# A list of kernel steps searched anew, and warm-up products of 256 instead of 512 columns

## The chip, the cores and the metric

The kernel runs on one core of a Trainium2 chip. The core's engines work side by side, each through its own queue in order: PE (matrix products; PEld is its loading of weights), DVE (vector operations), ACT (scalar functions and copies), POOL and SP. SP has no arithmetic here; it issues most of the transfers. The metric is the time of the program on the device in microseconds. Three runs of the kernel before took 153.74, 154.20 and 155.04 us, a median of 154.2.

## What is computed

Two models see the same input x (2048 positions of 512 values), and a gate mixes them:

```python
def _A_ref(x, ...):                    # state space: 512 complex states
    Lam_bar = jnp.exp(dt * Lam)
    Bu = jnp.einsum("bld,pd->blp", x + 0j, B_bar)
    for t in range(L):
        h = Lam_bar[None, :] * h + Bu[:, t, :]
    y = 2.0 * jnp.einsum("blp,dp->bld", hseq, Cmat).real + x * Dskip
def _B_ref(x, wqkv, w_phi, wo):        # linear attention: 32 heads of 16
    phi_q = concat(softmax(pq), softmax(-pq)); phi_k = the same of pk
    kv = einsum("bhsf,bhsd->bhfd", phi_k, v); z = sum of phi_k over s
    o = (phi_q @ kv) / (phi_q . z + 1e-6)
    return o.reshape(B, S, D) @ wo
g = sigmoid((x * gate_w).sum(-1, keepdims=True))
return g * a + (1 - g) * b
```

## The kernel before

The kernel has no scheduler that decides while it is built. It is written as some 190 small generators, called steps, and a string `ORDER` names them one after the other. A loop at the end reads the string: each token runs its generator up to the next `yield`, and what it issues there goes to the end of the queue of its engine. So the string is the order of every instruction on every engine. A token may carry the numbers of the PSUM banks that it takes (`k5@6`) and a `D` (`f0:D`), which sends a copy or a scaling to DVE instead of ACT. The banks are eight, with 2 KB in each partition. When a bank or a buffer is used again, the framework adds the wait for the earlier user; so it does between any two engines that use one bank.

The steps that the text speaks of:

- `Z` (L333 to L337): a product of zeros with zeros that nobody reads. It keeps PE busy in the head while the first loads are on their way.
- `Lk`, `Lx`, `Lv`, `Lb`, `Lq`, `Lc` (L226 to L259): loads, each issued by SP: rows of the key weights (two; the rest comes through ACT's queue at L159), two natural x tiles (L232) and seven transposing x loads of two tiles each (L236), value weights, state space matrices B, query weights, C.
- `W` (L315 to L323): key weights transposed by PE, and copied out; `f` (L469 to L479): four folds of them with the feature map, each ended by a copy; `w` the same for the queries. `T` (L325 to L331): transposes of the two natural x tiles.
- `V`, `P`, `U`, `P2` to `P4`, `M`, `i`: parameters of the state space, small vector operations on DVE with a few sines and exponentials on ACT.
- `k`, `v`, `q` (L528 to L551): projections of a tile of 128 positions, four products each, with a copy by ACT behind them (L135, the line of the helper `evac`). A `q` has three tokens: products, copy, and a DVE operation (L550) that takes the gate column from the same bank, as `nge`.
- `x`, `n`, `e`, `s` and `X`, `N`, `E`, `S`: the two softmaxes of up to four tiles: maxima and differences, minima and differences (DVE), exponentials (ACT, L589), sums and scaling (DVE); `S` ends with transposes by DMA. `a` adds keys times values on PE.
- `b`, `g`, `z`, `sa`, `sb`, `H`, `XX`, `hd`, `hk`, `ek`, `dp`: the state space, as products over strides of the sequence and corrections. `z` scans (L720) and multiplies again (L723); `c` scales C, `C` stores it turned.
- `y`, `o`, `O`, `t`, `R`: output of a tile. `y` is the state space's product, `o` the attention's with its division (L891), `O` its transpose by DMA (L904), `t` the product with `wo` into the same bank as `y` and the copy out (L922), `R` the store.

What a `q` does behind its four products, and `Z`:

```python
        evac(xrel(n), pq[:, 0:DF].rearrange("p (hh x) -> p hh x", hh=8))
        yield
        VS(out=nge[:, n:n + 1], in0=pq[:, DF:DF + 1], scalar1=-Z_MAX, scalar2=-1.0, op0=ALU.max, op1=ALU.mult)
        yield
```

Of the kernel before, what the change touches and what calls it, by code (L numbers as in the profile page):

```python
# [23 lines left out]
ORDER = """
Z@0 B Lx Lk Z Lk B Z Z B Z T0@1 T0 W01@2 Z W00@3 W00 Lx W10@1 W11@4 Lv B W10 Z W01 W11 Z T1@1 B f3@0 W00 T1:D W01 Lx
f2@3 V@2 f0@4 V Lx f3 P f1@5 f1 f0:D P P2 v0@1 P2 P2 Lb f2 k0@4 P2 P2 P U v1@5 k0 P4 V2@3 P3 P2 U k1@0 P4 k1 U k2@2
P4 P3 i i k0 k1 M i M v0 Lx k4@4 x0 i Lx k3@1 n0 x0 k7@0 n0 M i M2 Lb Lx V2 k5@6 k6@3 n0 x0 Lq Da k4 v3@4 x0 k2 k3
M2 n0 k9@1 x0 n0 i k11@2 x1 k8@7 k6:D L n1 x1 k5 n1 e0 k10@3 Da v3 x1 Lq n1 w2@4 k7 k9 v1 s0 Lb Lx n1 Db x1 k8 s0 w2
x1 U n1 Lb w3@1 x2 s0 k11 x2 Lx v6@0 w1@7 b10@5 n2 v6 M2 e1 w0@2 x2 s0 k10 n2 x2 s0 b01@0 b31@4 b30@6 n2 x2 w3 Lc n2
Db x0z s0 b00@3 g10@1 w0 k13@2 b30 x3 n2 b01 g00@0 x3 Da Lo s1 b10 Db b00 k13 w1 e2 g00 k14@2 Lc s1 n3 s1 k12@7 v5@3  # L30
g01@5 k12 g31@7 s0 g30@6 g30 gw e2 g00 c0:D s1 g10 x3 n3 b31 s1 g30 s2 Da Lc b20@4 k15@6 s1 g31 s2 k14 g10 a0@12 g01
c0:D c1 b20 x3 Lc a0 n3 k15 c2:D g01 v5 q3@0 c2:D s2 Lb g31 x3 c1:D q2@3 n3 c2 g31 x4 g01 s2 q3 x4 v2@6 g01 q2 s2 q2
g31 q3 n3 v4@4 g01 s2 s1 g20@0 n4 x4 g31 n4 v2 e3 Ld b21@3 g20 s2 a1 g31 b11@6 g31 c0:D s2 n4 g20 g01 a1 g31 b21 c3
q0@0 g11@3 v4 g21@4 b11 q0 g01 g11 g01 c3:D g31 q1@7 e3 q1 g11 x4 n4 g01 c0 x4 q6@6 q6 g21 q1 a2 g21 c3 s3 q0 b40@5
g11 n4 b50@0 g11 g21 c2 g21 v7@7 b40 g11 N0 g21 Lb X0 g11 a2 b50 s3 v10@0 g21 X0 q4@5 c1 g11 g21 v10 c1 g11 v7 N0 Ld
s3 a2 g21 g50@0 g11 a2 q4 g50 N0 g21 c3 q7@4 s3 z0@3 G0 X0 e4 z0 X0 s3 q5@7 N0 e4 q6 C g40@6 q4 q5 b70@5 X0 z0 C q5
N0 q7 C z0 s4 z0 g40 b60@3 b70 b71@7 b51@5 g40 q7 z0@4 b71 N1 z0 z0 s4 b41@7 X1 g70@4 z0 X1 b60 s3 g50 b41 g41@0 E0
b51 sa0@7 g60@3 s4 g70 sa0 sb0@7 s3 g60 s4 g71@5 sb0 E0 g41 g51@6 H0@7 s4 X1 g51 g70 g51 s4 S0 H0 C g71 H1@4 S0 X1
g60 g41 XX0 S0 g51 hd0 g41 H1 g71 G0 g51 b61@7 g71 N1 S0 v8@3 s4 g71 v9@4 b61 G1 g51 g61@7 G1 v8 XX0 g51 g41 g61 hd0
N1 a3 v9 g61 g71 s3 g71 g41 g41 a3 S0 v11@4 a3 g51 Ld hd1 g51 g41 S0 g61 g61 S0 g71 q10@3 v11 hd0 g61 g61 s4 a3 g71  # L40
XX0 N1 XX0 q10 g71 g41 g61 q11@4 g41 g61 v12@0 S0 g61 g51 z1@6 S0 q11 X1 N1 z1 hd0 z1 q8@7 q10 q8 q9@5 z1 q8 q13@3
q11 z1 v14@4 z1@7 v12 q9 q9 z1 S0 E1 E1 a4 hd1 X2 N2 z1 q12@5 v15@7 G0 G1 z1 N2 X2 N2 sa1@0 v13@6 sa1 q15@0 v13
sb1@6 S1 v14 hd0 v15 X2 S0 a4 S1 sb1 q14@4 H2@7 q12 G2 H3@6 S1 X2 q12 q14 hd1 S1 a4 q13 S1 H2 hd1 q14 a4 q13 Y Y Y
hd1 S1 hk4 S1 y1@5 Y END y0@3 o0@1 q15 y2@4 H3 N2 X2 o1@6 hk6 q15 o1 o1 XX1 o0 N2 hd0 y3@0 o0 o0 o1 y1 XX1 hk5 XX1
o3@1 o2@6 hd1 E2 o2 y3 X3 y2 o3 XX1 S1 o2 o3 hk4 S1 o2 y1 y0 o3 N3 hk5 E2 hk7 hk4 O0 y0 X3 S1 t0 y4@1 hk5 X3 t0 hk6
y2 hk5 hk7 X3 S2 hk4 t1 y3 hk7 o4@2 o5@6 N3 ek0 S2 t1 o5 o4 O1 o5 t2 y7@5 t3 hk6 S1 S2 hk7 S2 o4 o4 N3 o5 O2 t2 ek0
y5@4 N3 o7@6 hk6 S2 S2 o6@2 y4 y4 t3 ek1 ek3 y5 S2 ek0 X3 o6 dp6@0 y7 S2 y5 ek1 ek2 N3 o6 o7 ek0 o6 R1 t4 t5 ek1 ek2
o7 E3 o7 y6@2 ek3 t4 y7 S2 dp6 y6 ek1 S2 ek2 ek3 ek2 E3 o8@0 o8 ek3 ek6:D o8 ek4:D ek4 o9@6 o9 y6 t5 ek6:D ek7 ek4
o9 O3 y11@3 S3 o8 ek6 ek5 ek5 S2 t7 R0 R2 o9 t6 y10@4 y9@0 ek7 t6 O4 ek4 ek5 o10@6 o10 o10 ek7 ek5 y8@1 ek6 ek7 y11
dp1@2 S3 o10 S3 dp1 y9 o11@6 t7 G2 S3 G2 y8 o11 dp3@2 dp2@5 o11 o11 S3 t8 S3 dp7@6 dp0@7 O5 S3 dp2 S3 dp5@5 dp0 dp3  # L50
t9 dp5 y10 y14@2 S3 S3 dp4@5 S3 u8 t11 dp7 y12@7 u9 t10 dp4 o12@5 o12 t8 R3 o12 t9 u10 y12 y12 o13@0 R4 o12 t10 y14
o13 o13 y14 o13 o15@5 u11 y13@4 o15 o15 o14@0 o14 o15 y13 O6 G3 o14 O8 G3 y15@56 y13 t11 y15 o14 O7 y15 t13 t12 R5
G3 t12:D t13 R6 t14 t15 t14 R7 t15 R8 t15 t15:D R8
"""
# [20 lines left out]
def kernel(  # L75
# [237 lines left out]
    MM = nc.tensor.matmul  # L313
# [17 lines left out]
        yield  # L331

    def st_Z():  # L333
        pz = bank([P, D], F32, "pz")
        while True:
            MM(out=pz[:], lhsT=warm[:, 0:P], rhs=warm[:], start=True, stop=True)
# [664 lines left out]
```

## Time and profile before

| | |
|---|---|
| median of three runs | 154.2 us (153.74 to 155.04) |
| the profiled execution | 153.31 us |
| its span, first to last instruction | 151.6 us |
| instructions | 2814 |
| PE products | 978 |
| moved by DMA | 19.73 MB in 54109 packets |
| read from and written to HBM | 3.56 MB and 2.10 MB |
| granted TensorE clock, mean | 0.997 |

A row of the profile names a line of the kernel, the engine, the operation, and what it writes and reads; then the count and the time. A matrix product is pipelined: its row's duration is longer than the distance to the next one, so the busy time of PE is not its speed. An arrow `<-` behind an idle time names what ended it. A wait is put down to what came last by the profile.

### The profile page before, as it was taken

The page shows a single profiled execution, that of the slowest core. Times are in us where ns is not written, and L with a number is a line of the kernel's source. Part 1 is how long each engine was busy: PE and PEld are TensorE (multiplying, and loading weights), DVE is VectorE, ACT ScalarE, POOL GpSimd, SP SyncE. Part 2 cuts the span into 40 slices and gives each one's busy share as a digit, 9 for nine tenths or more (in the row PEclk, how much of TensorE's full clock was granted, in tenths as well). Part 3 has the DMA queues.
Part 4 walks back from the last instruction along what each step waited for, and adds up shares of the span by engine and source line. Part 5 has one row for each costly group of instructions (what it writes and reads, how often), then busy time and mean ns, then how long its engine had stood idle before and what let it go on. Part 6 is the DMA issues. An engine that isn't in the chain of part 4 may idle for free.

```text
span 151.6 us, 2814 instructions
## 1 busy us (share of the span) xinstructions
PE 141.1 (93%) x978; PEld 72.6 (48%) x978; DVE 135.7 (89%) x334; ACT 122.1 (81%) x239; POOL 19.5 (13%) x47
## 2 busy tenths in 40 slices
PE   6799999999999999979999999899998999989990
PEld 2444444444535555434556455445553554436640
DVE  2679999999999999699999999999999999999620
ACT  3599999999999999969898899999999994003240
POOL 7700885000000000000030006300000000000000
PEclk9999999999999999999999999999999999999998
DMA  3999999998200000910355924989968993797543
GB/s 74 318 231 210 188 181 199 232 196 159 74 0 0 0 0 5 237 41 0 76 132 88 213 49 69 161 155 200 181 38 192 210 198 62 106 181 203 104 119 123
DMA packets 54109, 19.73 MB, mean 130 GB/s; under 512 B 44496, under 2 KB 54096, under 8 KB 54096
## 3 DMA queue, kind: packets, MB, share of 16 engines
q1 hardware_dynamic: 51904, 18.19, 60.3%
q0 software_dynamic: 1248, 1.06, 4.7%
q10 hardware_dynamic: 944, 0.31, 0.8%
q8 instruction: 7, 0.11, 0.3%
q14 instruction: 6, 0.05, 0.1%
HBM read 3.56 MB, written 2.10 MB: 37 GB/s over the span
## 4 chain that ended last, share of the span: by engine, by line
PE 37%; DVE 34%; DMA 11%; ACT 10%; issue 4%; SPq 1%; DVEq 0%
PE PS L860 9%; PE PS L516 7%; DMA oT<-on 6%; PE PS L916 6%; DVE sm L566 5%; PE PS L643 5%; DVE mx L566 4%; ACT EE L589 4%; DVE mn L566 3%; DVE EE L583 3%; PE PS L648 3%; DVE on L891 3%; ACT Xq L135 3%; DMA CS<-in_B_wqkv_dram 3%; DVE EE L577 3%
## 5 line engine op out<-in xcount | busy, mean ns | idle before, releaser
L589 ACT ACTIVATE EE<-EE 128x2048 bf16<-128x2048 bf16 x16 | 30.6, 1918 | 0.7 <-DVE EE L583 0.6
L516 PE MATMUL PS<-WKV,xT 128*128 128x512 bf16 (+1 forms) x128 | 29.6, 373 | 0.0
L516 PEld LDWEIGHTS <-xT 128*128 128x128 bf16 x192 | 18.1, 98 | 18.0 <-DMA xT<-in_A_x_dram 0.4
L860 PE MATMUL PS<-C,LS 128*128 128x512 bf16 (+1 forms) x104 | 24.0, 362 | 0.0
L135 ACT CAST Xq<-PS 128x480 bf16<-128x480 f32 x31 | 17.1, 578 | 1.2 <-PE PS L516 1.1
L916 PE MATMUL PS<-Wo,oT 128*128 128x512 bf16 (+2 forms) x68 | 15.7, 367 | 1.3 <-DMA oT<-on 1.2
L643 PE MATMUL PS<-xT,BT 128*128 128x512 bf16 x64 | 15.8, 379 | 0.1
L648 PE MATMUL PS<-xT,BT 128*128 128x512 bf16 x64 | 15.5, 380 | 0.0
L516 PE MATMUL PS<-Wq,xT 128*128 128x481 bf16 x64 | 15.4, 367 | 0.1
L135 ACT CAST LS<-PS 128x512 bf16<-128x512 f32 x24 | 13.5, 602 | 1.3 <-PE PS L648 1.1
L860 PEld LDWEIGHTS <-LS 128*128 128x128 bf16 x104 | 9.3, 98 | 8.8 <-issue 0.2
L684 POOL DMA_DIRECT2D LS<-CT x4 | 4.9, 1220 | 66.0 <-DVE EE L604 51.6
L882 ACT ACTIVATE ld<-PS 128x32 f32<-128x32 f32 x16 | 2.8, 190 | 11.6 <-PE PS L877 11.6
L891 DVE TENSOR_TENSOR on<-PS,rd 128x512 bf16<-128x512 f32 x16 | 10.9, 692 | 0.6 <-ACT rd L885 0.6
L922 ACT ACTIVATE ot<-PS,G 128x512 bf16<-128x512 f32 (+1 forms) x11 | 7.3, 665 | 4.4 <-PE PS L916 4.4
L577 DVE TENSOR_TENSOR EE<-Xq,mx 128x2048 bf16<-128x2048 bf16 (+1 forms) x9 | 10.4, 1151 | 0.1
L465 ACT ACTIVATE CT<-CS,nsn 128x512 bf16<-128x512 bf16 x15 | 10.4, 721 | 0.0
L465 ACT ACTIVATE CT<-HH,dgs 128x512 bf16<-128x512 bf16 x14 | 10.0, 723 | 0.3 <-DVE HH L735 0.3
L916 PEld LDWEIGHTS <-oT 128*128 128x128 bf16 x68 | 6.2, 98 | 8.3 <-DMA oT<-on 2.1
L566 DVE TENSOR_TENSOR sm<-EE 128x2048 bf16<-128x2048 bf16 (+1 forms) x9 | 9.9, 1105 | 0.0
L583 DVE TENSOR_TENSOR EE<-mn,Xq 128x2048 bf16<-128x2048 bf16 (+1 forms) x9 | 9.9, 1096 | 0.0
L648 PEld LDWEIGHTS <-BT 128*128 128x128 bf16 x64 | 6.1, 98 | 7.8 <-issue 1.2
(183 smaller groups left out, 273.4 us busy)
## 6 DMA issues: line engine op xcount, KB each, us to landing
out_dram<-ot SPq DMA_DIRECT2D x7, 256.0 KB, 2.9
C<-CS SPq DMA_DIRECT2D x4, 256.0 KB, 4.4
CS<-HH SPq DMA_DIRECT2D x8, 128.0 KB, 3.4
LS<-CT POOLq DMA_DIRECT2D x4, 256.0 KB, 5.0
WKV<-in_B_wqkv_dram SPq DMA_DIRECT2D x1, 512.0 KB, 5.2
C<-in_A_B_re_dram SPq DMA_DIRECT2D x1, 512.0 KB, 5.1
C<-in_A_B_im_dram SPq DMA_DIRECT2D x1, 512.0 KB, 5.0
Wo<-in_B_wo_dram SPq DMA_DIRECT2D x1, 512.0 KB, 4.8
```

Source lines behind the costliest of these rows:

```text
L135: nc.scalar.copy(out=out_ap, in_=in_ap)
L465: nc.scalar.mul(out=out_ap, in_=in_ap, mul=s_)
L516: MM(out=pt[:], lhsT=xT[:, kt, ti * P:(ti + 1) * P], rhs=W[:, kt, 0:pt.shape[-1]], start=(kt == 0), stop=(kt == KT - 1))
L566: VT(out=dst, in0=cur[:, :, :, 0:n, :], in1=cur[:, :, :, n:2 * n, :], op=op)
L577: VT(out=half(EE, 0), in0=X5, in1=live["mx", p].to_broadcast([P, L, 8, Dh, 4]), op=ALU.subtract)
L583: VT(out=half(live["EE", p], 1), in0=live["mn", p].to_broadcast([P, L, 8, Dh, 4]), in1=X5, op=ALU.subtract)
L589: aexp(out=EE[:, l_:l_ + 2], in_=EE[:, l_:l_ + 2], func=ACT.Exp)
L643: MM(out=pt[:], lhsT=BT[:, m, kt, :], rhs=cells(kt, r), start=(kt == 0), stop=False, skip_group_check=True)
L648: MM(out=pb[:], lhsT=BT[:, m, kt, :], rhs=cells(kt, 2 * pr), start=(kt == 0), stop=(kt == KT - 1))
L860: MM(out=py[:], lhsT=hs[m], rhs=C2[:, m, c:c + w], start=(m == 0), stop=False)
L891: VT(out=live["on", g_][:, u], in0=pn[:, :, :, 0:Dh], in1=rd[:].unsqueeze(3).to_broadcast([P, 2, 16, Dh]), op=ALU.mult)
L916: MM(out=py[:], lhsT=oT[:, g, :], rhs=Wo[:, g, c:c + w], start=False, stop=(g == HG - 1))
```

## The change

It has two parts. The string `ORDER` is replaced as a whole: the list of steps was searched anew by annealing over six draws of noise, with the order of two engines' reads of one bank taken into account. And the product of `Z` has 256 columns instead of 512, with 16 tokens instead of 8. All other steps occur as often as before. The list sets `D` otherwise for some steps: no longer on `T1`, `k6`, four single scalings of C (one of `c1`, two of `c2`, one of `c3`), two scalings of `ek6`, and `t12`; now on `T0`, `W10`, `f3`, one single scaling in `c1` and the double one in `c2`, one scaling of `ek5`, and `t14`.

```diff
 ORDER = """
-Z@0 B Lx Lk Z Lk B Z Z B Z T0@1 T0 W01@2 Z W00@3 W00 Lx W10@1 W11@4 Lv B W10 Z W01 W11 Z T1@1 B f3@0 W00 T1:D W01 Lx
-f2@3 V@2 f0@4 V Lx f3 P f1@5 f1 f0:D P P2 v0@1 P2 P2 Lb f2 k0@4 P2 P2 P U v1@5 k0 P4 V2@3 P3 P2 U k1@0 P4 k1 U k2@2
-P4 P3 i i k0 k1 M i M v0 Lx k4@4 x0 i Lx k3@1 n0 x0 k7@0 n0 M i M2 Lb Lx V2 k5@6 k6@3 n0 x0 Lq Da k4 v3@4 x0 k2 k3
...
-s3 a2 g21 g50@0 g11 a2 q4 g50 N0 g21 c3 q7@4 s3 z0@3 G0 X0 e4 z0 X0 s3 q5@7 N0 e4 q6 C g40@6 q4 q5 b70@5 X0 z0 C q5
-N0 q7 C z0 s4 z0 g40 b60@3 b70 b71@7 b51@5 g40 q7 z0@4 b71 N1 z0 z0 s4 b41@7 X1 g70@4 z0 X1 b60 s3 g50 b41 g41@0 E0
...
+Z@0 Lk Lk Z Z Z B Z Z B Z Z Z Lx Z Z W01@2 Z W00@3 Z B Z W00 Z B W01 W10@1 W00 Lx B W10:D W11@4 Lx W01 Z f0@2 f1@5
+T1@1 W11 T0@4 f0:D f1 Lv T1 f2@3 f3@0 Lx Lx T0:D f2 V@2 V k1@5 P k0@4 f3:D P Lx P2 P k0 P2 P2 U P2 k1 P2 U P3 P4 k0
+k1 U k2@2 P3 P4 k3@1 n0 v0@5 P4 x0 k5@6 k2 v1@2 Lb Lq n0 i x0 P2 k7@0 v3@4 i V2@3 k3 x0 v0 k5 i n0 i k9@1 x0 v1 i i
+Lq x0 n0 Lb k7 M n0 k8@7 k4@0 M k6@2 n1 M Lx w2@6 x1 w0@5 V2 v6@3 x0z Lx n1 x1 v3 n1 L Da Lx Lb Lb x1 Lb Da Lb e0 n1
...
+q7@0 c1 g11 q6 N0 b50 z0@6 c3 Lo z0 b70@1 v7 a2 q4 s3 z0 q4 q5@5 q7 a2 e4 q6 s3 q7 b70 q5 X0 e4 N0 z0 a2 c3 X0 b71@3
+z0 g40@6 X0 b61@1 N0 z0@0 b71 g50@2 b61 g50 g50 q5 z0 z0 b51@5 X1 c3 v10@0 g40 s4 b60@3 z0 sa0@2 g70@1 b51 g61@5 N0
...
     def st_Z():
-        pz = bank([P, D], F32, "pz")
+        pz = bank([P, 2 * P], F32, "pz")
         while True:
-            MM(out=pz[:], lhsT=warm[:, 0:P], rhs=warm[:], start=True, stop=True)
+            MM(out=pz[:], lhsT=warm[:, 0:P], rhs=warm[:, 0:2 * P], start=True, stop=True)
             yield
```

Of the orders on the other queues, SP's is the one the text uses. Its first fourteen transfers before: x tile, two rows of key weights, x tile, value weights, two x transposes, B real, two x transposes, B imaginary, x transpose, two halves of the query weights. After: two rows of key weights, two x tiles, x transpose, value weights, three x transposes, B real, two halves of the query weights, B imaginary, x transpose; behind them come two more x transposes and all four transposes of B.

More of the change, by code (lines that the diff above doesn't have):

```diff
@@ L24 @@
 ORDER = """
-Z@0 B Lx Lk Z Lk B Z Z B Z T0@1 T0 W01@2 Z W00@3 W00 Lx W10@1 W11@4 Lv B W10 Z W01 W11 Z T1@1 B f3@0 W00 T1:D W01 Lx
-f2@3 V@2 f0@4 V Lx f3 P f1@5 f1 f0:D P P2 v0@1 P2 P2 Lb f2 k0@4 P2 P2 P U v1@5 k0 P4 V2@3 P3 P2 U k1@0 P4 k1 U k2@2
-P4 P3 i i k0 k1 M i M v0 Lx k4@4 x0 i Lx k3@1 n0 x0 k7@0 n0 M i M2 Lb Lx V2 k5@6 k6@3 n0 x0 Lq Da k4 v3@4 x0 k2 k3
-M2 n0 k9@1 x0 n0 i k11@2 x1 k8@7 k6:D L n1 x1 k5 n1 e0 k10@3 Da v3 x1 Lq n1 w2@4 k7 k9 v1 s0 Lb Lx n1 Db x1 k8 s0 w2
-x1 U n1 Lb w3@1 x2 s0 k11 x2 Lx v6@0 w1@7 b10@5 n2 v6 M2 e1 w0@2 x2 s0 k10 n2 x2 s0 b01@0 b31@4 b30@6 n2 x2 w3 Lc n2
@@ L30 @@
[L30 to L34, printed above, removed]
@@ L35 @@
-g11 n4 b50@0 g11 g21 c2 g21 v7@7 b40 g11 N0 g21 Lb X0 g11 a2 b50 s3 v10@0 g21 X0 q4@5 c1 g11 g21 v10 c1 g11 v7 N0 Ld
-s3 a2 g21 g50@0 g11 a2 q4 g50 N0 g21 c3 q7@4 s3 z0@3 G0 X0 e4 z0 X0 s3 q5@7 N0 e4 q6 C g40@6 q4 q5 b70@5 X0 z0 C q5
-N0 q7 C z0 s4 z0 g40 b60@3 b70 b71@7 b51@5 g40 q7 z0@4 b71 N1 z0 z0 s4 b41@7 X1 g70@4 z0 X1 b60 s3 g50 b41 g41@0 E0
-b51 sa0@7 g60@3 s4 g70 sa0 sb0@7 s3 g60 s4 g71@5 sb0 E0 g41 g51@6 H0@7 s4 X1 g51 g70 g51 s4 S0 H0 C g71 H1@4 S0 X1
-g60 g41 XX0 S0 g51 hd0 g41 H1 g71 G0 g51 b61@7 g71 N1 S0 v8@3 s4 g71 v9@4 b61 G1 g51 g61@7 G1 v8 XX0 g51 g41 g61 hd0
@@ L40 @@
[L40 to L53, printed above, removed]
+Z@0 Lk Lk Z Z Z B Z Z B Z Z Z Lx Z Z W01@2 Z W00@3 Z B Z W00 Z B W01 W10@1 W00 Lx B W10:D W11@4 Lx W01 Z f0@2 f1@5
@@ new lines @@
+T1@1 W11 T0@4 f0:D f1 Lv T1 f2@3 f3@0 Lx Lx T0:D f2 V@2 V k1@5 P k0@4 f3:D P Lx P2 P k0 P2 P2 U P2 k1 P2 U P3 P4 k0
+k1 U k2@2 P3 P4 k3@1 n0 v0@5 P4 x0 k5@6 k2 v1@2 Lb Lq n0 i x0 P2 k7@0 v3@4 i V2@3 k3 x0 v0 k5 i n0 i k9@1 x0 v1 i i
+Lq x0 n0 Lb k7 M n0 k8@7 k4@0 M k6@2 n1 M Lx w2@6 x1 w0@5 V2 v6@3 x0z Lx n1 x1 v3 n1 L Da Lx Lb Lb x1 Lb Da Lb e0 n1
+k4 w3@4 k6 k9 w3 x1 w0 x1 v6 k10@0 n1 k10 s0 x2 k11@2 s0 w1@4 k8 M2 e1 k13@1 k15@3 w1 Db x2 k15 b11@7 U x2 b10@5 k11
+b01@0 b20@4 n2 x2 Lc n2 b10 x2 n2 s0 w2 n2 M2 s0 k13 b00@3 n2 M2 g01@5 Da Db x3 g10@1 b30@6 s0 b01 b20 s0 Lc e2 Db
@@ new lines @@
+s1 b31@4 g10 g30@0 n3 b30 s0 c1:D x3 b00 g00@3 s1 g30 k12@6 c0:D b31 g00 g01 k14@2 e2 b11 a0@74 g00 gw a0 g01 g10 n3
+q1@1 s1 b21@3 n3 x3 s1 Da s1 x3 g30 v2@0 c0:D k12 n3 s1 q3@6 k14 q0@2 g01 s2 x3 n3 s2 q1 q1 b21 Lc c0:D q2@3 n4
+g11@1 x4 e3 g11 g11 q3 v2 g31@0 g01 s1 x4 q3 g20@6 g31 q0 q0 a1 q2 n4 s2 x4 e3 g31 g20 c0 g11 g01 n4 c2 g01 g31 a1
+g01 g20 s2 g21@2 x4 q2 g11 s3 Lc g21 c2 g21 g11 s2 v5@3 g01 g21 c1 v5 g31 g21 s2 x4 v4@6 g21 s3 c2:D g31 s3 b40@3
+g01 g11 v4 g21 n4 s3 g31 g21 s3 g31 v7@5 b50@6 b40 g21 g31 n4 g11 s2 q6@3 X0 N0 G0 c1 g21 s2 X0 g11 a2 q4@2 c2 g31
@@ new lines @@
+q7@0 c1 g11 q6 N0 b50 z0@6 c3 Lo z0 b70@1 v7 a2 q4 s3 z0 q4 q5@5 q7 a2 e4 q6 s3 q7 b70 q5 X0 e4 N0 z0 a2 c3 X0 b71@3
+z0 g40@6 X0 b61@1 N0 z0@0 b71 g50@2 b61 g50 g50 q5 z0 z0 b51@5 X1 c3 v10@0 g40 s4 b60@3 z0 sa0@2 g70@1 b51 g61@5 N0
+X1 b60 g71@3 s4 g71 g70 v10 g51@0 c3 sa0 X1 g40 sb0@2 Ld s4 s3 N1 g60@6 sb0 N1 s4 g51 g61 g51 N1 E0 E0 C g60 C g70
+g51 S0 v11@2 s4 G1 N1 G0 v8@1 g60 Ld S0 g51 H1@6 g61 v11 s4 v8 X1 S0 b41@2 v9@1 g51 H1 S0 s4 hd1 C g51 s4 a3 S0 g71
+v9 g41@6 a3 b41 g41 H0@2 g41 a3 a3 hd1 G0 g71 g51 C S0 g71 g61 g41 G1 S0 g71 g61 H0 g41 XX0 g41 q9@2 g61 g71 hd0 G1
@@ new lines @@
+g51 g51 g61 g71 g41 g61 q10@1 X1 g61 XX0 g41 N1 q9 g71 g41 g61 q8@0 g71 g41 S0 hd1 z1@6 q8 q10 z1 S0 z1 q11@3 q9 q11
+v13@6 z1 q10 E1 q8 E1 z1 v12@0 XX0 z1@1 X2 N2 v14@2 q14@5 v13 q11 v12 z1 z1 X2 XX0 v15@1 N2 q12@3 z1 v15 hd0 v14 S0
+S0 N2 hd1 hd1 hd0 hd1 q14 S1 a4 N2 S1 X2 sa1@0 a4 S1 sa1 a4 q12 a4 sb1@6 S1 q13@0 Y Y sb1 S1 hd0 q15@7 Y X2 H2@6 Y
+o0@1 q14 G2 S1 END q15 X2 XX1 y1@5 q15 hd0 q13 q12 S1 o0 o1@3 H3@7 N2 y1 H3 o1 H2 hd0 o3@6 XX1 XX1 o0 q13 o0 o1 E2
+E2 o1 N3 S1 XX1 y3@0 hk4 S1 o2@1 y2@4 y0@3 y2 O0 o2 y0 S1 y0 S2 o3 X3 o2 hk6 y1 o3 hk4 hk7 o2 t1 t0 y3 o3 hk7 hk6
@@ new lines @@
+y4@1 y2 S2 hk4 hk5 O1 t0 S2 o5@6 X3 S2 y3 hk4 hk7 S2 N3 t1 X3 S1 o4@2 S2 y6@5 hk5 X3 t2 S2 o5 ek0 hk5 hk7 R0 S2 o4
+o5 o4 ek0 t3 hk5 hk6 t2 o4 ek3 ek3 o5 t3 o6@2 S2 N3 S2 hk6 X3 N3 o6 o7@6 y5@4 ek0 o7 o6 N3 o6 O2 o7 o7 ek2 ek1 y5 y4
+y6 S2 dp5@0 ek1 y4 ek3 y5 dp6@2 o8@6 dp6 dp5 y6 E3 t4 ek2 Ld o9@2 o8 ek0 y7@0 o9 y7 ek2 ek1 o8 t5 o8 o9 ek2 o9 ek1
+ek4:D E3 o10@6 t4 y7 o10 O3 o11@2 ek5 S3 t7 ek3 o10 t6 ek6 o11 ek4 o11 O4 y10@1 o10 S3 G2 dp1@6 ek5:D y11@7 t6 t7 t5
+o11 ek5 S3 O5 ek7 ek6 ek4 ek5 ek7 S3 dp0@2 ek6 R2 ek7 ek4 y9@0 ek6 ek7 S3 dp7@4 y8@3 dp2@5 S3 dp2 y10 y8 dp3@5 t8
@@ L54 @@
+y11 S3 R1 S3 dp7 dp4@4 G2 dp1 u8 S3 S3 S3 t11 t8 G3 dp0 t10 y9 t9 o13@2 dp3 o13 o12@5 o12 u9 dp4 t9 R3 y14@4 y12@0
+u10 o12 G3 y14 o12 o13 o15@5 o13 o15 y12 o15 o14@2 t10 o14 G3 y12 o14 u11 o15 y13@1 O6 y13 t11 y15@56 y15 y13 t12
+t13 R4 R5 o14 O7 y14 t14 O8 t12 t13 R6 y15 t14:D R7 t15 t15 t15 R8 t15:D R8
 """
```

## The prediction

> **What bounds the kernel now.** I read the page first: the span, the busy times, and the shares of the chain of work that ended last.
>
> ```profile
> span 151.6 us, 2814 instructions
> PE 141.1 (93%) x978; PEld 72.6 (48%) x978; DVE 135.7 (89%) x334; ACT 122.1 (81%) x239; POOL 19.5 (13%) x47
> PE 37%; DVE 34%; DMA 11%; ACT 10%; issue 4%; SPq 1%; DVEq 0%
> ```
>
> The profiled execution took 153.3 us, 1.7 us more than its span; the median of the three runs, 154.2, is 0.9 us above that execution. PE and DVE share the chain almost evenly, so a shorter idle time on one of them helps only if the other follows. Next I read the busy times by stage (columns: window and width, busy us of PE, PE loads, DVE, ACT and POOL, granted clock, DMA).
>
> ```profile
> 0.00:6.50 6.50, 4.14 (x25) 1.93 (x26) 3.01 (x22) 2.10 (x3) 5.39 (x18) 1.00 0.62 189
> 6.50:14.00 7.50, 7.17 (x50) 3.78 (x49) 5.49 (x28) 7.06 (x16) 0.29 (x1) 1.00 1.21 229
> 14.00:18.00 4.00, 4.00 (x22) 1.89 (x20) 3.92 (x18) 3.93 (x7) 2.56 (x8) 1.00 1.06 215
> 18.00:60.00 42.00, 41.42 (x267) 20.58 (x266) 41.78 (x95) 41.03 (x77) 6.38 (x18) 1.00 0.52 96
> 60.00:70.00 10.00, 9.05 (x45) 4.05 (x44) 8.59 (x20) 8.77 (x13) 0.00 (x0) 1.00 0.43 106
> 70.00:96.00 26.00, 25.68 (x195) 14.03 (x194) 25.60 (x61) 24.14 (x53) 3.70 (x3) 1.00 0.54 99
> 96.00:128.00 32.00, 30.75 (x245) 16.36 (x244) 32.00 (x71) 29.95 (x60) 1.18 (x1) 1.00 0.88 159
> ```
>
> Width minus busy time is idle time. DVE idles 3.49 + 2.01 + 0.08 = 5.6 us up to 18, 0.2 up to 60, 1.4 up to 70, 0.4 up to 96, and nothing from 96 to 128: 7.6 us in all. Outside the head it is the engine that never rests, and PE falls behind where it waits for it. So I follow DVE's idle time, and ask at the end whether PE follows. The waits, longest in total (columns: us, times, longest), say what DVE and PE waited for:
>
> ```profile
> DVE nge L550 <- ACT Xq L135: 1.8, 3, 1.4
> PE PS L723 <- DVE nge L550: 1.0, 1, 1.0
> DVE xT L137 <- PE PS L472: 0.9, 1, 0.9
> DVE vec L343 <- PE PS L341: 0.8, 1, 0.8
> ```
>
> **The reads of one bank.** A q step puts 480 columns and one gate column into one bank; ACT copies the 480 (L135), then DVE takes the one (L550). DVE waits for ACT's read although it needs nothing of it. The timeline around the longest such wait (start, duration; idle time before in brackets):
>
> ```profile
> 60.85 1.94 ACT L589 ACTIVATE EE<-EE 128x2048 bf16<-128x2048 bf16 x1
> 62.65 1.04 ACT L135 CAST Xq<-PS 128x480 bf16<-128x480 f32 x2
> 63.27 0.16 DVE L550 TENSOR_SCALAR nge<-PS 128x1 f32<-128x1 f32 x1 [1.41 <-ACT Xq L135]
> 66.60 0.27 PE L723 MATMUL PS<-w,Sw 128*128 128x256 bf16 x1 [0.95 <-DVE nge L550]
> ```
>
> An exponential of 1.9 us stood before ACT's copy, DVE stood 1.41 us with its whole queue behind a 0.16 us read, and 3 us later PE stood for the scan that came late. I added up the work (start to start of each kind, from this trace) that stands ahead of each of these pairs on its own engine. In the old list DVE's read came after only 0.2 us more work than ACT's copy at the bad place, and 1.1 and 1.4 us more at the first two waited pairs. In the new list the smallest of these differences is 3.1 us. Up to 60 us both engines idle about as much (5.9 and 5.8 us by the windows); in the new list, with the gain in the head below, ACT idles some 1.7 us more than DVE, so about 1 us is spare and all three waits go: 1.8 us of DVE. Bounds: 1.4 us if the small ones stay, 0 if ACT slips by more than 1 us against DVE.
>
> **The head.** In the new list the two SP loads of the key weights go ahead of those of the natural x tiles, and the folds f0 and f1 go ahead of the x transposes.
>
> ```profile
> 3.40 0.61 PE L328 MATMUL PS<-ident,CS 128*128 128x128 bf16 x4
> 4.65 0.28 PE L319 MATMUL PS<-ident,CS 128*128 128x128 bf16 x2 [0.64 <-DMA CS<-in_B_wqkv_dram]
> 5.72 0.73 PE L319 MATMUL PS<-ident,CS 128*128 128x128 bf16 x10 [0.47 <-DMA CS<-in_B_wqkv_dram]
> 6.27 2.05 ACT L135 COPY Xq<-PS 128x512 bf16<-128x512 bf16 x4 [1.64 <-PE PS L319]
> 7.13 0.55 PE L472 MATMUL PS<-BD,Xq 128*128 128x120 bf16 x4
> 13.60 0.42 DVE L566 TENSOR_TENSOR mx<-Xq 128x512 bf16<-128x512 bf16 x1
> ```
>
> The first and second load of the SP queue are used at 3.40 and 4.65, the third at 5.72. With the weights first, ACT's copies of transposed weights start near 5.0 instead of 6.27; they are 0.5 us apart, so the first fold can run at 6.1 instead of 7.13. DVE now copies one weight block and f0 between its constants and the next x copy. That fills the 0.9 and 0.8 us it spent waiting for the x copy and for the parameters: 1.7 us of DVE, which then reaches the first minimum near 10.8 (13.60 before, but with some 2 us of table arithmetic ahead of it that is now mixed in behind). Bounds: 0.5 if the vector loads decide the second wait again, 2.2 if the next copies also close up.
>
> **The products of 256 columns.**
>
> ```profile
> 1.26 2.31 PE L336 MATMUL PS<-Drow 128*128 128x512 bf16 x5 [1.26 <-DVE Drow L156]
> 4.77 0.38 PE L336 MATMUL PS<-Drow 128*128 128x512 bf16 x1
> ```
>
> Sixteen of 256 columns are as many columns as eight of 512. Five took 2.31 us, 0.46 each, so the eleven now at the front take at most 11 x 0.23 = 2.5 us and end at 3.8, when the first weights are there. The second load (4.65) covers this 0.4 us; without that cover it would cost 0.4.
>
> [...]
>
> **Work moved between DVE and ACT.**
>
> ```profile
> L467 DVE TENSOR_SCALAR CS<-CT,csp 128x512 bf16<-128x512 bf16 x6 | 1.9, 337 | 0.0
> L467 DVE TENSOR_SCALAR CT<-HH,dgs 128x512 bf16<-128x512 bf16 x2 | 0.6, 352 | 0.0
> L467 DVE TENSOR_SCALAR CT<-CT,csp 128x1024 bf16<-128x1024 bf16 x1 | 0.5, 468 | 0.0
> L137 DVE COPY xT<-PS 128x512 bf16<-128x512 bf16 x1 | 0.4, 425 | 0.9 <-PE PS L472 0.9
> L465 ACT ACTIVATE CS<-CT,csp 128x512 bf16<-128x512 bf16 x2 | 1.5, 736 | 0.0
> ```
>
> DVE loses three CS products and one HH product and gains one double CT product and one copy: -3 x 0.34 - 0.35 + 0.47 + 0.43 = -0.5 us. ACT gains about 1 us net (three CS products at 0.74 are the most of it). ACT idles 1.0 + 1.2 + 1.9 + 2.1 = 6.1 us between 18 and 128, which hides it; uncovered it would cost that 1 us.
>
> **What is late next: the x loads.** The new list uses key tiles sooner, so PE asks for x sooner, and these loads come from one queue.
>
> ```profile
> 3.14 4.38 SPq L236 DMA_TRANSPOSE xT<-in_A_x_dram  x2
> 8.35 4.00 SPq L236 DMA_TRANSPOSE xT<-in_A_x_dram  x2
> 13.04 1.34 SPq L236 DMA_TRANSPOSE xT<-in_A_x_dram  x1
> 14.43 2.69 SPq L249 DMA_TRANSPOSE phT<-in_B_wqkv_dram  x1
> 22.17 0.49 PE L472 MATMUL PS<-BD,phT 128*128 128x120 bf16 x6 [0.36 <-DMA phT<-in_B_wqkv_dram]
> ```
>
> The queue is issuing all the time here, and the DMA share of the windows to 18 us is about 1. In the old list PE waited at 22.17 for the fourteenth SP transfer, the second half of the query weights. The first fourteen SP transfers are the same set in both lists (four small loads, the value weights, five x transposes, two B loads, two query loads), but in the new one the last of them is the fifth x transpose. So that lands near 22.1 as well. The new list asks for it after 56 x products and 28 fold products, the old one waited after 60 and 18; at 0.2 us each PE is there at about 20.5, and waits 1.6 us. PE's head start of 0.8 us is gone by that. DVE is passed this wait only as far as it has no distance from PE: summed work shows it 1.0 us behind PE's releases at an EE buffer near 38 us, and 0.2 us near 77, so the pace reaches DVE in steps. I take 1.8 us in all, nearest to the 1.6; bounds 0 (the load lands by 20.5, or the slack holds) and 3.5 (two of the transposes issue at 2.7 us, as at 14.43, instead of 1.3, as at 13.04).
>
> **Does the end follow?**
>
> ```profile
> 128.59 0.69 DVE on L891
> 129.31 4.91 DMA oT<-on
> 134.27 1.04 PE PS L916 x4
> 144.15 3.25 PE PS L916 x16
> ```
>
> This is the chain in order of time: from DVE's product at 128.59 through a transpose, and from 134.27 PE is never idle to the last product. If DVE is earlier at 128, the transpose and PE's last 13 us start earlier by the same amount. The work of PE, the transposes through SP and the output pieces at the end stay the same in number, and the summed work puts each of the late transposes as far ahead of its use as before, within 1 us.
>
> **The sum**, on the chain through DVE: -1.7 (head) - 1.8 (bank reads) - 0.5 (moved work) + 1.8 (x loads) = -2.2 us, 151.1 for an execution like the profiled one and 154.2 - 2.2 = 152.0 against the median.
>
> **Rivals.** (a) The x loads come in time, or the slack between PE and DVE takes the 1.6 us: no price, -4.0 us, 150.2. For it: DVE is fed by ACT's copies, which have reserves of over 1 us there. Against it: the queue is never free up to 22 us.
>
> (b) PE does not follow, or the head gains nothing: then the bank reads and moved work alone are left and the x loads take most of it, -1.8 - 0.5 + 1.8 = -0.5, 153.7. [...] The case in which the change does not do what it says belongs here too: the order of reads is met at these pairs, but ACT's slip makes new waits of the same 1.8 us.
>
> (c) Slower: the x loads are later by much. The new list has three x transposes in a row, then two query loads, then three x transposes and four BT in a row. In the old trace the second of two successive transposes issued in 2.6 to 2.9 us (4.38 for two at 3.14, less 1.4). If four of the pairs that are new pay 1.3 us more, the load that PE needs at 20.5 lands at 27: a wait of 6.5 us, of which the gain of 4.0 and the 0.2 to 1.0 us of distance take 4 to 5. That gives +2.0, 156.2. It turns slower than before beyond a wait of some 4.5 us, that is a landing after 25. [...]
>
> **Chances.** Forecast (151.0 to 153.3) 0.50; (a) 0.20; (b) 0.18; (c) 0.12. About 1%, 1.5 us, is what a measurement of this kernel can tell from no change; that puts the border of faster at 152.7 and of slower at 155.7. Some three quarters of the forecast's range and all of (a) are faster: 0.39 + 0.20. The rest of the forecast and most of (b) are no change: 0.11 + 0.16. Slower is (c) and a little of (b): 0.14. The range leaves out (c)'s upper part and little at the lower end of (a): 149.8 to 154.9.
>
> **What the new profile would show.** Bank reads: no wait of DVE nge for ACT Xq over 0.3 us. Head: the first fold before 6.5, the first minimum near 11, DVE idle to 18 us near 4. x loads: a wait of PE or its loads for xT between 20 and 23 us; none means (a), over 4 us means (c). End: DVE still without idle time from 96 to 125, and its last waits for oT no longer than before. The prediction is wrong if DVE's idle time falls by 2 us and PE's last product is not earlier, or if the idle time only moves to other waits for ACT.

## The result, and the profile after

The new list took 152.20 us (median of four runs, 151.96 to 152.28), the kernel before 154.01 beside it (four runs, 153.74 to 155.04). The ratio is 0.9868 with a 95% interval of 0.9819 to 0.9916: 1.3 us to 2.8 us of 154 faster, forecast 2.2. The profiled execution took 151.96 us, 1.35 less than the one before. One run below, of the list read early, was in a slower state of the chip and is left out of its median. The page of the new list:

```profile
span 150.2 us, 2835 instructions
PE 140.9 (94%) x986; PEld 75.2 (50%) x986; DVE 135.1 (90%) x332; ACT 121.9 (81%) x241; POOL 21.4 (14%) x47
PE 55%; DVE 24%; SPq 10%; DMA 7%; issue 1%; ACT 0%; DVEq 0%
```

The chain now lies more on PE (55% against 37%) and less on DVE (24% against 34%). The busy times of the new list in the same stages (window and width, busy us of PE, PE loads, DVE, ACT and POOL, granted clock, DMA):

```profile
0.00:6.50 6.50, 5.24 (x35) 4.07 (x36) 3.04 (x23) 2.69 (x4) 5.39 (x18) 1.00 0.76 165
6.50:14.00 7.50, 7.42 (x52) 4.11 (x51) 7.08 (x30) 6.49 (x16) 0.26 (x1) 1.00 0.98 231
14.00:18.00 4.00, 4.00 (x22) 1.77 (x20) 3.93 (x18) 3.97 (x8) 0.83 (x2) 1.00 1.35 146
18.00:60.00 42.00, 40.27 (x264) 20.58 (x263) 40.96 (x92) 39.65 (x77) 10.05 (x24) 1.00 0.48 99
60.00:70.00 10.00, 10.00 (x53) 4.69 (x50) 10.00 (x22) 10.00 (x14) 0.00 (x0) 1.00 0.04 10
70.00:96.00 26.00, 25.20 (x206) 14.10 (x205) 25.58 (x61) 25.18 (x58) 4.58 (x4) 1.00 0.71 142
96.00:128.00 32.00, 30.65 (x232) 16.07 (x231) 32.00 (x71) 30.01 (x60) 0.32 (x1) 1.00 0.88 171
```

Width less DVE's busy time (the third of the busy times) is DVE's idle time: 3.46 + 0.42 + 0.07 up to 18 us (3.95, before 5.58), then 1.04 (0.22), 0 (1.41), 0.42 (0.40) and 0 (0), 5.4 us in all against 7.6. The fall in the head and at 60 to 70 us is there, and 0.8 us of it is given back between 18 and 60 us. PE's idle time rises in that same stage from 0.58 to 1.73. The waits of the new list (total us, times, longest) say for what:

```profile
PEld L516 <- DMA xT<-in_A_x_dram: 1.8, 1, 1.8
PE PS L516 <- DMA xT<-in_A_x_dram: 1.7, 1, 1.7
DVE EE L577 <- PE PS L633: 0.8, 1, 0.8
```

PE stands once for a transposed x tile; DVE stands later for an EE buffer that PE has not yet released. No wait of DVE's gate read for ACT's copy is left in the list. The timeline of the new list (start, duration; idle time before in brackets) shows the places named in the prediction:

```profile
1.24 2.53 PE L336 MATMUL PS<-Drow 128*128 128x256 bf16 x11 [1.24 <-DVE Drow L156]
...
5.06 1.03 PE L319 MATMUL PS<-ident,CS 128*128 128x128 bf16 x10
...
5.09 1.63 ACT L135 COPY Xq<-PS 128x512 bf16<-128x512 bf16 x3 [1.96 <-PE PS L319]
6.21 0.74 PE L472 MATMUL PS<-BD,Xq 128*128 128x120 bf16 x8
...
10.64 0.43 DVE L566 TENSOR_TENSOR mn<-Xq 128x512 bf16<-128x512 bf16 x1
...
22.57 1.79 PE L516 MATMUL PS<-WKV,xT 128*128 128x480 bf16 x8 [1.65 <-DMA xT<-in_A_x_dram]
...
57.77 0.59 ACT L135 CAST Xq<-PS 128x480 bf16<-128x480 f32 x1
58.40 0.22 DVE L550 TENSOR_SCALAR nge<-PS 128x1 f32<-128x1 f32 x2
```

ACT's copy ends at 58.36 and DVE's read of the same bank starts at 58.40: the order holds here, but with nothing to spare. The chain of the new list at its end (start, duration, in order of time):

```profile
113.59 1.21 DVE on L891 x2
115.99 4.20 DMA oT<-on
120.24 1.90 PE PS L916 x8
...
144.14 0.86 PE PS L916 x4
```

Before, the chain left DVE for the last time at 128.59 and PE's last wait ended at 134.27. Now PE has no idle time after 120.24 that the chain shows. Was PE alone the bound from there? That was my first theory for the tail, and the experiments threw it out.

### The profile page after: what moved, and what is told of

The parts are those of the page before. It is cut to its first block, busy times and chain, and to the rows that moved or that the text cites. A ratio compares the mean times of both kernels' runs of the same rounds, so it can differ in the third digit from the quotient of the medians.

```text
span 150.2 us, 2835 instructions
## 1 busy us (share of the span) xinstructions
PE 140.9 (94%) x986; PEld 75.2 (50%) x986; DVE 135.1 (90%) x332; ACT 121.9 (81%) x241; POOL 21.4 (14%) x47
## 4 chain that ended last, share of the span: by engine, by line
PE 55%; DVE 24%; SPq 10%; DMA 7%; issue 1%; ACT 0%; DVEq 0%
PE PS L516 12%; PE PS L860 9%; PE PS L648 9%; PE PS L643 9%; PE PS L916 6%; SPq L236 5%; DMA xT<-in_A_x_dram 4%; DVE on L891 3%; DVE sm L566 3%; SPq L249 3%; DMA oT<-on 3%; PE PS L660 2%; DVE EE L577 2%; DVE EE L616 2%; DVE HH L735 2%; DVE EE L583 2%
## 5 line engine op out<-in xcount | busy, mean ns | idle before, releaser
L516 PE MATMUL PS<-WKV,xT 128*128 128x480 bf16 (+1 forms) x128 | 29.6, 373 | 1.7 <-DMA xT<-in_A_x_dram 1.7
L860 PE MATMUL PS<-C,LS 128*128 128x512 bf16 (+1 forms) x104 | 23.0, 363 | 0.0
L135 ACT CAST Xq<-PS 128x480 bf16<-128x480 f32 x32 | 17.6, 584 | 1.7 <-PE PS L516 1.7
L135 ACT CAST LS<-PS 128x512 bf16<-128x512 f32 x24 | 14.1, 630 | 0.9 <-PE PS L648 0.7
L465 ACT ACTIVATE CT<-HH,dgs 128x512 bf16<-128x512 bf16 x15 | 10.7, 718 | 0.2 <-DVE HH L735 0.2
L891 DVE TENSOR_TENSOR on<-PS,rd 128x512 bf16<-128x512 f32 x16 | 10.8, 710 | 0.0
L135 ACT CAST vx<-PS 128x512 bf16<-128x512 f32 x16 | 9.9, 633 | 0.1
L604 DVE TENSOR_TENSOR EE<-EE,rc 128x2048 bf16<-128x2048 bf16 x8 | 9.7, 1219 | 0.1
```

The lines of the kernel that those rows point to most:

```text
L135: nc.scalar.copy(out=out_ap, in_=in_ap)
L465: nc.scalar.mul(out=out_ap, in_=in_ap, mul=s_)
L516: MM(out=pt[:], lhsT=xT[:, kt, ti * P:(ti + 1) * P], rhs=W[:, kt, 0:pt.shape[-1]], start=(kt == 0), stop=(kt == KT - 1))
L860: MM(out=py[:], lhsT=hs[m], rhs=C2[:, m, c:c + w], start=(m == 0), stop=False)
L891: VT(out=live["on", g_][:, u], in0=pn[:, :, :, 0:Dh], in1=rd[:].unsqueeze(3).to_broadcast([P, 2, 16, Dh]), op=ALU.mult)
```

## The experiments

The kernels ran in three groups, each group on one chip with its own runs of the kernel before. Medians, and ratios to the kernel before with 95% intervals:

| run | median us | ratio | interval |
|---|---|---|---|
| new list again | 152.10 | 0.9890 | 0.9848 to 0.9933 |
| old list, ACT's copy first | 152.75 | 0.9924 | 0.9900 to 0.9949 |
| new list, read early | 152.65 | 0.9937 | 0.9910 to 0.9963 |
| new list, x before B imaginary | 151.57 | 0.9865 | 0.9831 to 0.9899 |
| new list, x tile first | 152.08 | 0.9899 | 0.9860 to 0.9938 |
| new list, constant products of 512 | 151.89 | 0.9885 | 0.9850 to 0.9919 |
| new list, less PE at the end | 151.85 | 0.9874 | 0.9842 to 0.9907 |
| old list, less PE at the end | 153.98 | 1.0013 | 0.9982 to 1.0044 |
| new list, less DVE at the end | 152.13 | 0.9884 | 0.9853 to 0.9915 |
| new list, less of both | 150.98 | 0.9809 | 0.9782 to 0.9835 |
| new list, x before both B | 151.75 | 0.9857 | 0.9825 to 0.9889 |
| new list, scalings of C back to DVE | 152.76 | 0.9901 | 0.9864 to 0.9938 |

The kernel before had medians of 153.76, 153.76 and 153.95 in the three groups. An interval is 0.8 to 1.3 us wide, so differences of 0.3 us between rows are not told apart, and one of 0.6 us is at the border. A diff of `ORDER` below shows the changed stretch of a line, not the whole line.

**The new list unchanged**, as the yardstick of the first group:

> The new list unchanged, as the control of this call. Expected: 152.2 us (151.9 to 152.4), ratio to the kernel before 0.983 to 0.992.

It came out at 152.10, 1.7 us under its neighbour.

**Undoing the worst read of one bank in the old list.** One exponential is moved behind the copy that DVE's read waited for, and nothing else:

```diff
-q5@7 N0 e4 q6 C g40@6 q4 q5 b70@5
+q5@7 N0 q6 C g40@6 q4 q5 e4 b70@5
```

> The old list with one token moved: the second exponential of the fifth key group (e4) goes behind the copy of q5 instead of ahead of it, so that DVE's read of that bank no longer waits for a copy that stands behind 1.9 us of exponential. Theory (DVE's idle time counts at the end in the old list, and this wait was a loss of its own): the wait of 1.41 us goes, the time falls by 1.0 to 1.5 us, to about 152.8. Rival (the later waits for the transposes of the outputs end last anyway, so this wait was hidden): within 0.3 us of the kernel before, 153.7 to 154.3.

Measured: 1.0 us faster than before, with an interval (0.8 to 1.5 us) that excludes no change. The timeline of this kernel at the place where DVE had stood 1.41 us:

```profile
62.09 0.56 ACT L135 CAST Xq<-PS 128x480 bf16<-128x480 f32 x1 [0.16 <-PE PS L516]
62.55 1.91 ACT L589 ACTIVATE EE<-EE 128x2048 bf16<-128x2048 bf16 x1
62.72 0.14 DVE L550 TENSOR_SCALAR nge<-PS 128x1 f32<-128x1 f32 x1
```

The copy is now ahead of the exponential, and DVE reads without a wait. DVE's idle time between 60 and 70 us falls from 1.41 to 0.29 us. (In this execution PE's products stayed long until past 9 us, eight folds taking 0.83 us at 9.23 where eight took 0.59 at 8.47 before, and DVE idled 0.94 us more up to 18 us; the span is 0.4 us shorter all the same.) By the medians, one token moved gives more than half of what the whole new list gives.

**Putting such a wait into the new list.** DVE's last gate read of that group is moved eleven tokens ahead (the expectation says nine steps):

```diff
-z0 g40@6 X0 b61@1 N0 z0@0 b71 g50@2 b61 g50 g50 q5 z0 z0
+q5 z0 g40@6 X0 b61@1 N0 z0@0 b71 g50@2 b61 g50 g50 z0 z0
```

> The new list with one token moved: DVE's read of q5's gate column goes nine steps ahead, to where ACT's copy of the same bank is not done yet, so that DVE waits about 1.3 us there (60.6 to 61.9 us). Theory (DVE's idle time before 115 us counts at the end): 0.9 to 1.4 us slower than the new list, about 153.3. Rival (PE is the bound in the new list from 22 us on and DVE has room): within 0.3 us of the new list, 151.9 to 152.5.

Measured: 0.6 us slower than the new list beside it by the medians, between the two expectations; the intervals of the two overlap. The timeline of this kernel shows the wait that was put in:

```profile
62.16 0.62 ACT L135 CAST Xq<-PS 128x480 bf16<-128x480 f32 x1
62.81 0.16 DVE L550 TENSOR_SCALAR nge<-PS 128x1 f32<-128x1 f32 x1 [1.16 <-ACT Xq L135]
```

DVE stands 1.16 us, as it did before the change, and the median grows by half of that. Together: 1.4 us of wait removed gave 1.0, 1.2 us put in cost 0.6. The medians are each uncertain by some 0.5 us. That such a wait costs time is shown in the old list, at 0.8 to 1.5 us for 1.4; in the new list the sign is likely and the price is not settled. In both traces a read of 0.16 us waits out a copy whose data it doesn't use: 1.16 us here, 1.41 in the kernel before.

**The head.** One of the two natural x tiles goes ahead of the key weights, as in the old list:

```diff
-Z@0 Lk Lk Z Z Z B Z Z B Z Z Z Lx Z Z W01@2
+Z@0 Lx Lk Lk Z Z Z B Z Z B Z Z Z Z Z W01@2
```

> The new list with one of the two natural x tiles loaded ahead of the two key-weight rows, as in the old list; nothing else moved. If the earlier start of the weight copies is what shortened the head, ACT's first copy of transposed weights starts some 0.5 us later, DVE idles 0.5 to 1 us more before 18 us, and the time is 0.5 to 1.0 us above the new list's. The rival: from 20 us on PE waits for its x load in any case, and a later head only shortens that wait: within 0.3 us of the new list, with the wait of the products of L516 for xT shorter by what the head lost.

Measured: 152.08 against 152.10. The first fold ran 1.1 us later, and PE waited less for x; from the timeline of this kernel:

```profile
7.30 1.01 PE L472 MATMUL PS<-BD,Xq 128*128 128x120 bf16 x8
...
22.84 1.79 PE L516 MATMUL PS<-WKV,xT 128*128 128x480 bf16 x8 [0.52 <-DMA xT<-in_A_x_dram]
```

The x tile lands at 22.52 us in the new list and at 22.79 here, while PE comes for it at 20.92 and at 22.32. And DVE's idle time only changes its place, as the windows of this kernel show:

```profile
6.50:14.00 7.50, 7.45 (x54) 5.12 (x53) 5.52 (x24) 6.03 (x13) 0.26 (x1) 1.00 1.00 229
18.00:60.00 42.00, 41.32 (x259) 20.96 (x261) 41.84 (x97) 40.74 (x79) 10.86 (x25) 1.00 0.49 99
```

DVE idles 1.98 us between 6.5 and 14 (new list 0.42) and 0.16 between 18 and 60 (new list 1.04, and 1.71 in its second profile). Up to 18 us it idles 5.50 us, nearly the 5.58 of the old list, so the gain in the head is undone almost whole. That gain is real as idle time of DVE, and nothing of it can be told in the time, because the next thing that both engines need comes through SP at a time of its own. The intervals leave room for a cost of up to some 1 us, not for the 1.7 us of the forecast.

**The x loads.** First one x transpose is moved ahead of B imaginary:

```diff
-Lq x0 n0 Lb k7 M n0 k8@7 k4@0 M k6@2 n1 M Lx w2@6
+Lq x0 n0 Lx Lb k7 M n0 k8@7 k4@0 M k6@2 n1 M w2@6
```

> The new list with one load moved: the fifth x transpose goes ahead of the load of the imaginary part of B instead of behind it. Theory (PE's wait of 1.8 us at 22.6 is the load's place in SP's queue, and its price was passed on in part: DVE's wait of 0.8 us at 38.7): x lands near 20 us, the wait at 22.6 falls below 0.4 us, DVE's wait at 38.7 goes, the time falls by 0.5 to 1.0 us, to 151.2 to 151.7. Rival 1 (the price was taken up by slack before the end): the wait goes and the time stays within 0.3 us. Rival 2 (the transposes of B, which need that load, are late in its place): a new wait of PE for BT near 26 us of over 1 us, and no gain or a loss of up to 1 us.

Then, in a later group, B real goes behind it too (the diff is against the new list):

```diff
-k2 v1@2 Lb Lq n0 i
+k2 v1@2 Lq n0 i
...
-Lq x0 n0 Lb k7 M n0 k8@7 k4@0 M k6@2 n1 M Lx w2@6
+Lq x0 n0 Lx Lb Lb k7 M n0 k8@7 k4@0 M k6@2 n1 M w2@6
```

> The new list with one x transpose ahead of B imaginary, as in the run that had that alone, and B real moved behind it too, so that the query weights and the x transpose each leave SP 0.7 us sooner and the two loads of B stand together. If PE's wait between 19 and 24 us sets the pace, the waits for the query weights and for x together fall from 1.5 us in that run to 0.8, and the time by 0.3 to 0.7 us against it, 151.0 to 151.3. The rival: the transposes of B then wait for their load, PE stands before L648 near 30 us for as much, and the time is that run's or worse.

Measured: the median is 0.5 us under the new list beside it, and about the same for the second (its ratio is 0.9857 against 0.9865). The timelines of the two kernels, SP's transposes and PE's wait, the first kernel first:

```profile
15.78 2.56 SPq L236 DMA_TRANSPOSE xT<-in_A_x_dram  x1
...
19.04 3.98 SPq L236 DMA_TRANSPOSE xT<-in_A_x_dram  x2
...
24.24 1.90 PE L516 MATMUL PS<-WKV,xT 128*128 128x480 bf16 x8 [1.24 <-DMA xT<-in_A_x_dram]
```

```profile
12.96 1.60 SPq L236 DMA_TRANSPOSE xT<-in_A_x_dram  x1
...
16.52 6.01 SPq L236 DMA_TRANSPOSE xT<-in_A_x_dram  x2
...
23.75 1.92 PE L516 MATMUL PS<-WKV,xT 128*128 128x480 bf16 x8 [1.19 <-DMA xT<-in_A_x_dram]
```

In the first kernel PE's wait does not go, as I had expected, but moves. The load that PE stood for lands at 20.41 us instead of 22.52, and PE now stands 1.24 us for the next one, which lands at 24.19. DVE's later wait for the EE buffer stays too (0.9 us, 0.8 in the new list). So the time lies in the range that I gave, and not for the reason that I gave. In the second kernel that next load, the first of the last two, is issued 2.5 us sooner (16.52 instead of 19.04), but it lands 7.2 us after its issue instead of 5.2, at 23.70. PE's wait ends at 23.75 instead of 24.24. Here the order moved the arrival by a fifth of what it moved the issue. The two loads of B stand directly ahead of it now; whether they are the cause no run shows by itself. I had expected 0.3 to 0.7 us from the second edit and it gave nothing that can be told. These two have the lowest medians of the kernels that leave nothing out, but their intervals overlap the new list's, so neither is shown to be faster than it.

**The constant products** with 512 columns and half as many tokens:

```diff
-        pz = bank([P, 2 * P], F32, "pz")
-            MM(out=pz[:], lhsT=warm[:, 0:P], rhs=warm[:, 0:2 * P], start=True, stop=True)
+        pz = bank([P, D], F32, "pz")
+            MM(out=pz[:], lhsT=warm[:, 0:P], rhs=warm[:], start=True, stop=True)
```

> The new list with the constant products at 512 columns and every second of their tokens left out, so that as many columns pass through the array. [...]

Measured: 151.89, the same as the new list within what can be told. The folds took as long as in one execution with the short products: eight at 6.37 us took 0.89 us here, and 0.88 at 6.34 there (the run with the scalings of C back on DVE).

**The end.** Six products of the attention's output are left out, of the new list and of the old one:

```diff
-            for g in range(HG):
+            for g in range(HG - 1 if n in (8, 9) else 0, HG):
```

> The new list with six of the eight products of the attention's output with wo left out for tiles 8 and 9 (one product of four stays in each): 6 products of 0.216 us, 1.3 us of PE between 128 and 133 us, and no other work. If PE is what sets the end from 120 us on, as the chain of waits of the new list shows, the time falls by 1.1 to 1.4 us against the new list. If the end hangs on DVE or on the transposes through SP, it falls by less than 0.4 us.

> The old list with the same six products left out (tiles 8 and 9, 1.3 us of PE near 130 us). In the old list PE waits for a transposed attention tile until 134.27 us, behind DVE's product at 128.59, and these six products lie ahead of that wait. So the saving is swallowed by the wait: within 0.3 us of the old list. If instead PE sets the end here too, the time falls by 1.1 to 1.4 us.

Less PE in the new list: 0.25 us under the new list's 152.10, not the 1.1 to 1.4 of my theory. In this kernel PE, freed of 1.3 us, runs into a wait at 133.5; its timeline:

```profile
132.50 0.38 PE L916 MATMUL PS<-Wo,oT 128*128 128x512 bf16 x1
133.51 0.68 PE L877 MATMUL PS<-KVm,phT 128*128 128x68 bf16 x16 [0.63 <-DVE xd L896]
```

and its waits name the transfer that came last for the loading of weights:

```profile
PEld L877 <- DMA phT<-EE: 1.1, 1, 1.1
```

These are the transposed features of the last query group. In the unchanged new list (its second profile) SP issues them from 128.61 on, and PE reaches their use at 133.87, without a wait:

```profile
128.61 4.88 SPq L620 DMA_TRANSPOSE phT<-EE  x2
...
133.87 0.67 PE L877 MATMUL PS<-KVm,phT 128*128 128x68 bf16 x16
```

The first of the two transposes is the one that PE needs here. It lands 4.7 us after its issue, at 133.35, some 0.5 us before PE uses it; in the run with less PE it landed at 133.46, which is when PE's wait ended. So two chains would stand abreast: PE's products, and DVE's scaling with the transposes behind it. The chain of waits shows only the later one. That became the next theory, and the two products of DVE were left out, alone and together with those of PE:

```diff
-            VT(out=em, in0=em, in1=rho[:, u * NB:(u + 2) * NB].to_broadcast([P, 2 * NB, Dh, 4]), op=ALU.mult)
+            if p != "G3":
+                VT(out=em, in0=em, in1=rho[:, u * NB:(u + 2) * NB].to_broadcast([P, 2 * NB, Dh, 4]), op=ALU.mult)
```

> The new list without the two products that scale the last query group's negative features (L616 of group 3, at 127.85 and 130.37 us): 1.2 us of DVE, and the transposes of that group can leave SP 0.6 us earlier. Theory, after the run with less PE: at 133.6 us PE and the transposed features of this group arrive within 0.3 us of each other, so either alone buys little: within 0.3 us of the new list. The rival, DVE alone sets the end: 0.6 to 1.2 us less.

> Both left out of the new list: the six products with wo of tiles 8 and 9 (1.3 us of PE) and the two scalings of the last query group (1.2 us of DVE). If PE and the chain through DVE and the transposes stand abreast at 133.6 us, the two together give what neither gives alone: 0.7 to 1.2 us less than the new list, where the run with less PE gave 0.3. The rival, the end hangs on something else (a third chain, the stores): less than 0.4 us again.

Less DVE alone gave nothing (152.13); less of both gave 150.98, 1.15 us under the run with less DVE beside it, and no run of the one overlaps a run of the other (150.84 to 151.13, and 151.77 to 152.68). Less PE alone ran in another group; by the ratios, less of both is 1.0 us under it. With less DVE alone the first transpose is issued at 126.30 and lands at 132.31, but PE has its own products to do until 133.48. With less of both the transpose lands at 132.66, and PE uses it at 132.71. The timelines of the two runs, less DVE first:

```profile
133.48 0.68 PE L878 MATMUL PS<-KVm,phT 128*128 128x68 bf16 x16
```

```profile
126.64 5.99 SPq L621 DMA_TRANSPOSE phT<-EE  x2
...
132.71 0.68 PE L878 MATMUL PS<-KVm,phT 128*128 128x68 bf16 x16
```

In each run with less on one side only, the other side sets when PE goes on; with less on both, PE goes on some 1 us sooner (132.71 against 133.63 and 133.87 in the two profiles of the new list), which is what the time shows.

In the old list the same six products bought nothing (153.98 against 153.76), as expected: the wait for oT that ended at 134.27 before takes up much of what they free. The timelines, the kernel before first:

```profile
134.27 1.04 PE L916 MATMUL PS<-Wo,oT 128*128 128x512 bf16 x4 [0.69 <-DMA oT<-on]
```

```profile
134.61 1.04 PE L916 MATMUL PS<-Wo,oT 128*128 128x512 bf16 x4 [1.18 <-DMA oT<-on]
```

**Scalings of C back to DVE.** Three tokens get a `D`, which is 1.0 us more of DVE and 2.2 us less of ACT between 47 and 52 us:

```diff
-g20 c0 g11 g01 n4 c2 g01 g31 a1
+g20 c0 g11 g01 n4 c2:D g01 g31 a1
...
-s3 Lc g21 c2 g21 g11 s2 v5@3 g01 g21 c1 v5
+s3 Lc g21 c2:D g21 g11 s2 v5@3 g01 g21 c1:D v5
```

> The new list with three scalings of C (one product CS from CT of 0.34 us each on DVE, 0.74 on ACT) given back to DVE, between 45 and 62 us: DVE gets 1.0 us more, ACT 2.2 us less; nothing else moves. The prediction priced moved work at one to one (0.5 us for 0.5): 0.8 to 1.0 us slower than the new list. If PE's own pace hides part of DVE's work, as the undone reads suggest (0.6 us of time for some 1.2 us of wait), 0.4 to 0.7. The rival, DVE does not bind in this stretch or ACT's relief pays it back: within 0.2 us.

Measured: 152.76, 0.6 us above the new list with less DVE at the end, which ran beside it and had come out like the new list. Its ratio, 0.9901, overlaps the new list's (0.9890). So 1.0 us of work given back to DVE cost 0.6 by the nearest pair of runs and 0.2 by the ratios. The single runs of that pair overlap (151.74 to 153.06, and 151.77 to 152.68), so neither sign nor size is settled.

## Why the prediction was right, point by point

**The reads of one bank** (forecast 1.8 us): right as a mechanism, and the largest part that a run shows. All three waits are gone, and undoing the worst alone in the old list gave 1.0 us of the 1.7 that the whole new list gives beside it. What makes up the other 0.7 us no run shows by itself. By the medians, a microsecond of wait costs less than one; the intervals don't exclude one.

**The head** (forecast 1.7 us): DVE's idle time to 18 us fell by 1.63, the first fold ran at 6.21 (forecast 6.1), the first minimum at 10.64 (10.8). As a term of the sum it was wrong: undone, it cost nothing that can be told.

**The x loads** (forecast +1.8): PE waited 1.65 us (forecast 1.6), for the load that I had named and at the place where I had put it; the rival with a landing at 27 us did not come, nor the one without a wait. But this term and the head are one. The wait exists because PE comes earlier to a load that doesn't. The sum had them with opposite signs and nearly the same size, so their total of +0.1 was right and neither of the two was worth what it said. That they cancelled so closely was in part luck: the sum gave them separate causes. What is left of the sum is the reads and the moved work, 2.3 us forecast, against 1.4 to 1.8 us measured.

**Moved work** (forecast 0.5): DVE's busy time fell by 0.6 us, 135.7 to 135.1. What this is worth in time is not shown: the run that gave work back doesn't settle it.

**The constant products** (forecast nothing): right. The eleven end at 3.77 (forecast 3.8), and 512 columns give the same time.

**The end follows DVE**: right in sign, and this is where the trace is furthest from my account. DVE's idle time to 128 us fell by 2.2 and its work by 0.6, yet the span fell by 1.4 and PE's last product ended 1.5 us sooner (145.89 instead of 147.40 by the chains). DVE then waits 5.3 us for PE's last products where it waited 2.96 before:

```profile
145.04 0.75 DVE L924 TENSOR_SCALAR ot<-PS,G 128x512 bf16<-128x512 f32 x1 [5.29 <-PE PS L916]
```

(timeline of the new list). The step that says that the transpose and PE's last 13 us start earlier by the same amount took one handover, at 128.59, for the only one. In the new list PE's own products fill the time from 120 us on, with DVE's scaling of the last features and their transposes just beside them. Whether the whole gain is 1.4, 1.7 or 1.8 us (profiled run, second group of runs, first) the runs don't settle; 2.2 lies inside both intervals.

**Longer products in the head** (an estimate of mine, 0.04 of the second rival): the trace does show them, and no cost of them can be seen. In the old list as profiled first, ten transposes at 5.72 took 0.73 us; in the new list ten at 5.06 took 1.03 and, in the run with the read early, 1.27. Whatever makes them longer, the x load covers it: in the run with the x tile first the folds at 7.30 still took 1.01 us, and the time was the new list's.

## What to carry to other kernels

When a change brings something forward, ask first what comes at a time of its own afterwards, and count the two together: a gain ahead of a late load and the wait for that load are one number, and undoing the gain shows it. Where two engines read one bank, let the long read be done well before the short one is due (here a read of 0.16 us cost DVE 1.41 us of waiting); the wait stands in the trace under the name of an engine whose data the reader doesn't use. Near the end, take work away from each of two chains alone and from both: if neither buys anything and both together do, they stand abreast, and a chain of waits that names one of them is not enough.
